# Loads of v issued from GpSimd's queue instead of SyncE's, in a fused top-k attention and Fourier-mixing kernel

## The chip, the core and the metric

The kernel runs on one core of one Trainium2 chip. A core has TensorE (PE in the profile), VectorE (DVE), ScalarE (ACT), GpSimd (POOL) and SyncE (SP). Each engine works through its own instruction queue in order and waits for the others through semaphores. PE, DVE, ACT and POOL compute; SP in this kernel only issues DMAs. The metric is the device time of one execution in microseconds (us), lower is better.

## What is computed

Inputs are q, k and v of shape (8, 8, 576, 64), that is 8 batches, 8 heads, 576 tokens and 64 channels of a head, and two weights. Cut to what matters:

```python
scores = scale * q @ k^T                        # per batch and head, 576 x 576
scores = where(scores >= 32nd largest of the row, scores, -1e9)
attn   = softmax(scores)
x      = (attn @ v), heads side by side         # (8, 576, 512)
u      = x + real(fft over channels(fft over tokens(x)))
un     = (u - mean(u)) / sqrt(var(u) + 1e-6)
out    = u + relu(un @ w_ch1) @ w_ch2           # hidden width 2048
```

All arithmetic is in float32.

## The kernel before

**Steps.** Two heads of one batch form a pair: 32 pairs, 4 of them to a batch (`NPB`). A pair has nine items (`PER_PAIR`, in the order of `IN_PAIR`), each 128 rows of scores with 576 columns; a pair's fifth item holds the leftover rows of both heads. The 288 items are run by one loop over steps `i` (line 1492). All instructions of a step are emitted in the order in which the loop meets them, and this order is the order in each engine's queue (the schedule is manual, line 1261). I call the step with `i % 9 == 7` "step 7 of a pair".

**An item's way.** VectorE finds the 32 largest values of a row in four rounds (`max`, line 425, and `match_replace`, line 427). At the end of the item's step GpSimd makes from them the two scalars `nt` (`bounds`, line 434). In the next step ScalarE forms a mask from the scores (line 448), GpSimd subtracts it from the scores (line 451), and ScalarE takes the exponential with a row sum (`expo`, line 459). From the second batch on, except in the last pair of the second batch and the last pair of all, the result goes through device memory: two ScalarE copies split its words (line 472), SP writes them out (`planes`, lines 485 and 488), and one step later SP issues a transposing DMA (`turn`, line 506) that brings them back as `PT`. TensorE multiplies `PT` with v (`attend`, line 564): a pair's first chunk four steps after its fifth item, so in step 8 of the pair; its second chunk four steps after the ninth, so in step 3 of the next pair. ScalarE then takes the product away (line 578).

**Around it.** Between these pieces the loop places the work of earlier batches: the Fourier stage (fold operations on GpSimd at lines 651 to 719; products on TensorE at lines 755, 812 and 816; ScalarE copies at lines 786 and 833; `add_mixed` on GpSimd at line 839; row statistics on VectorE at line 844; transposes on TensorE at line 881, each followed by a ScalarE copy at line 884) and the two matrix products of the channel network (TensorE lines 966, 993, 1032 and 1163; GpSimd sums at lines 1108 and 1135). A planner (`some`, `level`) spreads the TensorE part of this over the steps by estimated costs.

**The loads of v.** `v_t` holds two buffers that the pairs use in turn. `load_v(pair)` issues four DMAs, all on SP: two of 128 KB (line 288: 128 partitions, four runs of 256 bytes each) and two of 16 KB for the last 64 tokens (`load_tails`, line 255). In step 7 of a pair the loop calls `load_v` for the next pair, after the step's products and before `bounds` and the rest of GpSimd's work of the step. The first pair's v is loaded ahead of the loop. A buffer being loaded in step 7 was last read in step 3 of the same pair; what is loaded is first read in step 8 of the next pair.

**Queues around the call.** In step 7 SP's queue holds, in order: the transposing DMA of the item pair that the fifth item ends (`turn`), the write of item 5's planes, in some pairs the return of weight parts (line 909), then v's four loads, then stores if any. In step 8 follows the write of item 6's planes. GpSimd's queue holds in step 7: the subtraction of item 6, folds and sums if any, `nt` of item 7, sums, weight parts (line 923) or `add_mixed` if any. In step 8 it begins with the subtraction of item 7.

Of the kernel before, what the change touches and what calls it, by code (L numbers as in the profile page):

```python
# [73 lines left out]
def kernel(  # L74
# [9 lines left out]
    nc = tc.nc  # L84
# [11 lines left out]
    NPB = H // 2  # L96
# [129 lines left out]
    nat, qT_of, kT_of, v_of, PT, Ssb, Wk, Wp, M8, Nt = ({} for _ in range(10))  # L226
# [6 lines left out]
    def head_of(src, pair, e):  # L233
        b, hp = divmod(pair, NPB)
        return src[b, 2 * hp + e]
# [9 lines left out]
    def load_tails(dst, src, pair, queue=None, heads=(0, 1)):  # L245
        for e in heads:
            if src is q:
                for h in range(2):
                    (queue or nc.sync).dma_start(
                        out=dst[TH * h:TH * (h + 1), NF, e, :],  # L250
                        in_=head_of(src, pair, e)[HS * h + 2 * P:HS * (h + 1)],
                    )
            else:
                r0 = TAIL * e if src is v else 0
                (queue or nc.sync).dma_start(
                    out=dst[r0:r0 + TAIL, NF, e, :], in_=head_of(src, pair, e)[NF * P:S]
                )

    def load_nat(n, pair):
        if pair < NPAIR:  # L260
            nat[n, pair] = nat_t
            src = q if n == "q" else k
            b, hp = divmod(pair, NPB)
            both = src[b, 2 * hp:2 * hp + 2]
            if n == "k":
                for e in range(2):
                    nc.sync.dma_start(
                        out=nat_t[:, 0:NF, e, :],
                        in_=both[e, 0:NF * P].rearrange("(c p) d -> p c d", p=P),
                    )  # L270
                nc.sync.dma_start(
                    out=nat_t[0:TAIL, NF, :, :], in_=both[:, NF * P:S].rearrange("e r d -> r e d")
                )
                return
            for e in range(2):
                for h in range(2):
                    load_half(nat_t, src, pair, e, h)
            for h in range(2):
                nc.sync.dma_start(
                    out=nat_t[TH * h:TH * (h + 1), NF, :, :],  # L280
                    in_=both[:, HS * h + 2 * P:HS * (h + 1)].rearrange("e r d -> r e d"),
                )

    def load_v(pair):
        if pair < NPAIR:
            v_of[pair] = v_t[pair % 2]
            for e in range(2):
                nc.sync.dma_start(
                    out=v_of[pair][:, 0:NF, e, :],
                    in_=head_of(v, pair, e)[0:NF * P].rearrange("(c p) d -> p c d", p=P),  # L290
                )
            load_tails(v_of[pair], v, pair)

    def prep(n, pair, blocks=((0, NF), (NF, NC))):

# [31 lines left out]
    PER_PAIR = len(IN_PAIR)  # L327
# [4 lines left out]
    N = len(items)  # L332
# [74 lines left out]
    def top_ops(i, rounds):  # L407

        if not 0 <= i < N:
            return []  # L410
        if i not in Wk:
            e = items[i][2]
            if e != 1:

                if e is None:
                    Wp[i] = attp.tile([P, 1, S], F32, name=f"wk_{i}", tag="W1", bufs=1)
                else:
                    Wp[i] = attp.tile([P, 2, S], F32, name=f"wk_{i}", tag="W", bufs=3)
            Wk[i] = Wp[i - 1][:, 1, :] if e == 1 else Wp[i][:, 0, :]
            M8[i] = small.tile([P, TOPK], F32, name=f"m8_{i}", tag="m8", bufs=5)  # L420
        w, m, s = Wk[i], M8[i], Ssb[i]
        ops = []
        for r in rounds:
            src, m8 = s if r == 0 else w, m[:, 8 * r:8 * r + 8]
            ops.append(lambda src=src, m8=m8: nc.vector.max(out=m8, in_=src))  # L425
            if r < TOPK // 8 - 1:
                ops.append(lambda src=src, m8=m8: nc.vector.match_replace(w, m8, src, NEG))  # L427
        return ops
# [883 lines left out]
    for n in range(3):  # L1312
        load(n)
    load_v(0)
    load_nat("q", 1)
    for n in range(3, AHEAD):
# [123 lines left out]
    queue, waiting, pending, written, now, out_next = [], [], [], set(), [0], []  # L1440
    step_us = 6.0

    def chunk_at(i):

        for tile in (i - 4, i - 3, i - 2):
            r = tile % PER_PAIR
            if PER_BATCH <= tile < N and r in (4, 8):
                if i - tile == (4 if by_dma(tile) else 2 if tile == 2 * PER_BATCH - 1 else 3):
                    return tile // PER_PAIR, r // 8
        return None, None  # L1450
# [22 lines left out]
    def run(i, where):  # L1473
        for fn in plan.pop((i, where), []):
            fn()
# [15 lines left out]
    i, carry = 0, 0.0  # L1491
    while i < N + 5 or plan or queue or sums:
        now[0] = i
        run(i, "begin")
        pair_of = i // PER_PAIR
# [50 lines left out]
        if short:  # L1546
            fixed += tok
            pair, r = divmod(i - 1, PER_PAIR)
# [40 lines left out]
        pair, ch = chunk_at(i)  # L1589
# [8 lines left out]
        if i < N:  # L1598
            if q_step:
                load_nat("k", pair_of + 1)  # L1600
            if i % PER_PAIR == 5:
                load_nat("q", pair_of + 2)
            if i % PER_PAIR == 7:
                load_v(pair_of + 1)
        first, second = top_ops(i, (2, 3)), top_ops(i + 1, (0, 1))
        for n in range(max(len(first), len(second))):
            for ops in (first, second):
# [17 lines left out]
        run(i, "dve")  # L1625
        for where in ("pool", "pool2", "load", "load2"):
            run(i, where)
        late_now[:] = late_next
        late_next.clear()
        carry = max(-4.0, min(4.0, cost + got - step_us))  # L1630
# [37 lines left out]
```

## Time and profile before

| | |
|---|---|
| median of 3 runs | 1873.34 us (1872.83 to 1874.46) |
| the profiled execution's own time | 1868.68 us |
| its span, first to last instruction | 1866.9 us |
| mean granted TensorE clock | 0.955 of full speed |
| busy PE, DVE, ACT, POOL | 91%, 85%, 69%, 49% of the span |
| DMAs issued by SP for v | 64 of 128 KB and 64 of 16 KB |
| v's loads, issue to landing | 2.0 to 6.4 us |

The span has three parts. Up to about 240 us the weights arrive and the first batch's attention runs. From there to about 1690 us attention of a batch runs beside the Fourier stage and channel network of the one before; here TensorE and VectorE are both almost full (from 960 to 1200 us: 233.2 and 224.1 us busy of 240). The rest, to 1867 us, is the channel network of the last batch, almost all on TensorE. An engine's share of busy time does not tell how long others wait for it: GpSimd is busy half of the time, but a piece of each item's way lies on it.

### The profile page before, as it was taken

How to read it: one execution, taken by the hardware profiler on the slowest of the kernel's cores; microseconds unless marked ns; L12 is line 12 of the kernel's file. 1: busy time of each engine (PE TensorE's matmuls, PEld its weight loads, DVE VectorE, ACT ScalarE, POOL GpSimd, SP SyncE). 2: the span in 40 equal slices, each digit the busy share in tenths (PEclk: the TensorE clock that was granted, in tenths of full speed). 3: DMA queues.
4: the chain of work that ended last, by engine and by line, in shares of the span. 5: the costliest groups of instructions: out<-in, count | busy, mean ns of one | idle time of the engine just before them, and what ended most of it. 6: DMA issues, size and time to landing. Idle time of an engine off the chain costs nothing.

```text
span 1866.9 us, 26900 instructions
## 1 busy us (share of the span) xinstructions
PE 1704.1 (91%) x8134; PEld 1086.8 (58%) x8134; DVE 1584.9 (85%) x3301; ACT 1294.6 (69%) x3104; POOL 912.8 (49%) x1278
## 2 busy tenths in 40 slices
PE   5576699889899999899999999999999999999999
PEld 3344365365456555566556565666567555677677
DVE  7999989889899999999999899999999899762110
ACT  6878659577787778777787688767787678652100
POOL 4768644454745366354644465355545464341012
PEclk7777799899899999999999999999999999999999
DMA  5334016661567755586476755785467655530132
GB/s 168 104 92 115 20 45 162 168 176 26 129 157 202 188 128 130 147 208 160 118 169 169 188 127 139 154 230 133 128 162 189 161 121 146 133 106 6 51 112 72
DMA packets 516576, 249.16 MB, mean 133 GB/s; under 512 B 398288, under 2 KB 506448, under 8 KB 516432
## 3 DMA queue, kind: packets, MB, share of 16 engines
q1 hardware_dynamic: 515664, 247.23, 51.2%
q8 instruction: 65, 1.06, 0.2%
q14 instruction: 79, 0.65, 0.1%
q10 hardware_dynamic: 768, 0.21, 0.1%
HBM read 93.63 MB, written 84.74 MB: 96 GB/s over the span
## 4 chain that ended last, share of the span: by engine, by line
PE 61%; DVE 14%; POOL 7%; ACT 7%; DMA 4%; issue 4%; SPq 1%; POOLq 0%; DVEq 0%
PE hp L966 22%; PE cp L993 8%; PE o L564 7%; DVE m L425 6%; DVE wk L427 6%; PE sp L401 4%; PE cw L1163 4%; PE yp L755 3%; POOL wk L451 3%; PE cv L1163 3%; PE cp L1032 2%; PE sp_t L371 2%; ACT wk L448 1%; DMA PT<-planes 1%; DMA planes<-wk 1%
## 5 line engine op out<-in xcount | busy, mean ns | idle before, releaser
L451 POOL TENSOR_TENSOR wk<-S,wk 128x576 f32<-128x576 f32 x288 | 408.1, 1417 | 524.6 <-ACT wk L448 520.9
L425 DVE MAX8 m<-wk 128x8 f32<-128x576 f32 x864 | 626.8, 750 | 6.2
L966 PE MATMUL hp<-unT,w 128*128 128x256 f32 (+1 forms) x2048 | 528.3, 410 | 5.2 <-ACT unT L884 3.4
L966 PEld LDWEIGHTS hp<-unT,w 128*128 128x128 f32 x2048 | 381.3, 192 | 116.3 <-issue 10.1
L427 DVE MATCH_REPLACE8 wk<-m,wk 128x576 f32<-128x576 f32 x576 | 427.6, 742 | 0.0
L472 ACT COPY wk<-S 128x576 uint16<-128x576 uint16 x468 | 289.4, 669 | 0.0
L448 ACT ACTIVATE wk<-S,nt 128x576 f32<-128x576 f32 x288 | 223.2, 775 | 91.3 <-POOL nt L434 89.8
L564 PE MATMUL o<-PT,v 128*64 128x256 f32 (+3 forms) x1440 | 209.3, 437 | 34.7 <-DMA PT<-planes 18.6
L993 PE MATMUL cp<-w,hT 128*128 128x512 f32 x512 | 236.0, 601 | 0.0
L425 DVE MAX8 m<-S 128x8 f32<-128x576 f32 x288 | 213.8, 742 | 16.1 <-ACT S L375 16.1
L459 ACT ACTIVATE S<-wk,nt 128x576 f32<-128x576 f32 x234 | 184.5, 789 | 51.5 <-POOL wk L451 50.2
L427 DVE MATCH_REPLACE8 wk<-m,S 128x576 f32<-128x576 f32 x288 | 213.7, 742 | 0.0
L970 ACT ACTIVATE hT<-hp 128x320 f32<-128x320 f32 (+1 forms) x256 | 103.2, 411 | 146.0 <-PE hp L966 144.5
L564 PEld LDWEIGHTS o<-PT,v 128*64 128x64 f32 x1440 | 120.3, 160 | 113.4 <-issue 38.9
L401 PE MATMUL sp<-kT,qT 64*128 64x512 f32 (+1 forms) x528 | 169.0, 670 | 15.5 <-ACT S L393 7.7
L404 ACT COPY S<-sp 128x512 f32<-128x512 f32 (+1 forms) x264 | 141.8, 587 | 25.6 <-PE sp L401 24.7
L993 PEld LDWEIGHTS cp<-w,hT 128*128 128x128 f32 x512 | 93.3, 193 | 91.0 <-issue 90.5
L1108 POOL TENSOR_TENSOR hT<-hT 128x512 f32<-128x512 f32 x64 | 81.4, 1275 | 107.5 <-ACT hT L970 91.5
L434 POOL TENSOR_TENSOR nt<-m,cc 128x2 f32<-128x2 f32 x288 | 58.9, 204 | 142.0 <-DVE m L425 139.5
L371 PEld LDWEIGHTS sp_t<-kt,qT 128*128 128x128 f32 x320 | 50.6, 193 | 108.5 <-issue 69.8
L1163 PE MATMUL cw<-w,hT 128*128 128x256 f32 x448 | 104.7, 381 | 1.6 <-issue 1.6
L527 PE MATMUL tpP<-ident,wk 128*128 128x128 f32 x216 | 40.3, 318 | 58.9 <-ACT wk L459 34.1
(160 smaller groups left out, 2178.2 us busy)
## 6 DMA issues: line engine op xcount, KB each, us to landing
planes<-wk SPq DMA_DIRECT2D x208, 288.0 KB, 2.7
w<-w_parts SPq DMA_DIRECT2D x82, 512.0 KB, 4.7
space<-in_moe_w_ch_dram SPq DMA_DIRECT2D x32, 512.0 KB, 3.7
nat<-in_q_dram SPq DMA_DIRECT2D x128, 64.0 KB, 2.5
v<-in_v_dram SPq DMA_DIRECT2D x64, 128.0 KB, 3.0
out_dram<-x SPq DMA_DIRECT2D x32, 256.0 KB, 2.6
nat<-in_k_dram SPq DMA_DIRECT2D x62, 128.0 KB, 3.1
planes<-wk SPq DMA_DIRECT2D x52, 144.0 KB, 2.6
```

Of the source, the lines that this page charges most:

```text
L401: nc.tensor.matmul(sp[r], lhsT=qT[hd, q_cols], rhs=kT[hd, :], start=True, stop=True)
L404: nc.scalar.copy(out=s_t[r, keys], in_=sp[r])
L425: ops.append(lambda src=src, m8=m8: nc.vector.max(out=m8, in_=src))
L427: ops.append(lambda src=src, m8=m8: nc.vector.match_replace(w, m8, src, NEG))
L448: nc.scalar.activation(out=w, in_=Ssb[i], func=AF.Relu, scale=-FAR, bias=Nt[i][:, 1:2])
L451: nc.gpsimd.tensor_tensor(out=w, in0=Ssb[i], in1=w, op=ALU.subtract)
L459: nc.scalar.activation(out=Ssb[i] if by_dma(i) else w, in_=w, func=AF.Exp, bias=Nt.pop(i)[:, 0:1], accum_out=den_t[pair % 3][:, c:c + 1],)
L472: nc.scalar.copy(out=words[:, half, :], in_=src[:, half, :])
L564: nc.tensor.matmul(o[D * e:D * (e + 1), c0:c1], lhsT=vv[:, c, e, :], rhs=pt[:, NF if c == NF else (NF + 1) * e + c, c0:c1], start=(c == 0) ...
L966: nc.tensor.matmul(hp[:, 0:w], lhsT=w1[:, dt, P * it:P * (it + 1)], rhs=unT[:, dt, 0:w], start=(dt == 0), stop=(dt == NDT - 1),)
L993: nc.tensor.matmul(cp, lhsT=hT[:, it, P * n:P * (n + 1)], rhs=w2[:, it, :], start=(it == 0), stop=(it == NIT - 1),)
L1163: nc.tensor.matmul(dst, lhsT=h()[a][:, kc, :], rhs=rhs_of(kc), start=start and kc == 0, stop=kc == NK - 1, skip_group_check=True,)
```

## The change

From the fifth pair on `load_v` takes GpSimd's queue, and the call in the loop moves from the middle of step 7 to the end of it, behind all GpSimd work of that step. The first five pairs' v (pairs 0 to 4) still goes through SP; for pairs 1 to 4 the call is also the later one. So 27 pairs are concerned, with 4 DMAs each.

```diff
     def load_v(pair):
         if pair < NPAIR:
             v_of[pair] = v_t[pair % 2]
+            queue = nc.sync if pair <= NPB else nc.gpsimd
             for e in range(2):
-                nc.sync.dma_start(
+                queue.dma_start(
                     out=v_of[pair][:, 0:NF, e, :],
                     in_=head_of(v, pair, e)[0:NF * P].rearrange("(c p) d -> p c d", p=P),
                 )
-            load_tails(v_of[pair], v, pair)
+            load_tails(v_of[pair], v, pair, queue)
...
             if i % PER_PAIR == 5:
                 load_nat("q", pair_of + 2)
-            if i % PER_PAIR == 7:
-                load_v(pair_of + 1)
         first, second = top_ops(i, (2, 3)), top_ops(i + 1, (0, 1))
...
         for where in ("pool", "pool2", "load", "load2"):
             run(i, where)
+        if i < N and i % PER_PAIR == 7:
+            load_v(pair_of + 1)
         late_now[:] = late_next
```

The order of instructions on TensorE, VectorE and ScalarE stays the same. On SP 108 DMAs are gone. On GpSimd four DMAs stand behind the last instruction of step 7 and ahead of the subtraction of item 7, 27 times; the operations around them keep their order.

## The prediction

> **What bounds the kernel now.** I began with the stretches of the span, then took the list of waits, then the instructions in order of time around the places where v is loaded. The columns of the first view are the stretch, its length, then busy us (and instructions) of PE, PE's weight load, DVE, ACT and POOL, TensorE's granted clock, the DMA share and GB/s.
>
> ```profile
> 960.00:1200.00 240.00, 233.18 (x1122) 146.75 (x1121) 224.14 (x466) 185.60 (x441) 116.03 (x169) 0.99 0.62 158
> 1640.00:1866.00 226.00, 222.43 (x1031) 163.16 (x1027) 52.16 (x119) 46.93 (x117) 43.62 (x66) 1.00 0.20 66
> ```
>
> While attention runs, PE is 97% and DVE 93% busy, in lock step; after it PE alone. So a us by which PE or DVE is held up in the middle is a us at the end, unless PE would have waited later anyway. POOL has half its time free, but it stands in each item's way. In the waits (total us, times, longest) its idle time is time in which it waits for ACT, and ACT in turn waits for POOL:
>
> ```profile
> POOL wk L451 <- ACT wk L448: 520.9, 230, 9.3
> ACT wk L448 <- POOL nt L434: 89.8, 68, 4.0
> ACT S L459 <- POOL wk L451: 50.2, 49, 10.6
> ```
>
> The loads themselves hold up nobody. On SP no wait stands at lines 288 and 255, they land in 2.0 to 6.4 us, and they are read a whole pair (about 50 us) later. Line 1 of the next fence is from v's own view, line 2 too, line 3 from that of line 506 (min/median/max ns of one):
>
> ```profile
> L288 SPq DMA_DIRECT2D v<-in_v_dram x64: 419/562/1127, 8.0 to 1607.4; - x64
> L255 SPq DMA_DIRECT2D v<-in_v_dram x64: 513/595/773, 9.3 to 1608.6; - x64
> L506 SPq DMA_TRANSPOSE PT<-planes x130: 1294/2538/7724, 256.1 to 1629.1; - x130
> ```
>
> **What the change removes.** 27 times SP loses 2 x 0.562 + 2 x 0.595 = 2.31 us of issuing. I cost that at nothing. SP mostly waits (349.9 us for ACT's line 472, 202.6 us for planes to land). It is late behind v only in the last pair of a batch: in pair 23 v occupies SP from 1244.31 to 1246.85 and item 6's planes go out at 1246.96, although ACT had them at 1243.6. But the second chunk's last transposing DMA is issued at 1261.47, takes some 4.6 us, and the products that need it start at 1273.91: over 7 us of cover. Without that cover it would be 3.3 us a batch. One other use: in pair 5, SP sends a part of w2 (line 925) at 338.44, right after v, and POOL waits 10.8 us for it; it would come up to 2.6 us sooner.
>
> **What it adds, and where.** Four DMAs stand in POOL's queue between `nt` of item 7 and the subtraction of item 7, for which ACT's exponential waits, and behind that ACT's whole queue. Their waits (v's buffer read for the last time four steps before; the load two pairs back) are over by then. The place in pair 21, the second of its batch (start, length, engine, line, form, idle before):
>
> ```profile
> 1143.02 2.51 POOL L839 TENSOR_TENSOR x<-x,us 128x512 f32<-128x512 f32 x2
> 1145.49 1.41 POOL L451 TENSOR_TENSOR wk<-S,wk 128x576 f32<-128x576 f32 x1
> 1146.86 0.19 POOL L434 TENSOR_TENSOR nt<-m,cc 128x2 f32<-128x2 f32 x1
> 1147.78 2.52 POOL L839 TENSOR_TENSOR x<-x,us 64x512 f32<-64x512 f32 x2 [0.72 <-ACT us L833]
> ```
> ```profile
> 1148.06 0.83 ACT L459 ACTIVATE S<-wk,nt 128x576 f32<-128x576 f32 x1
> ...
> 1153.42 0.62 ACT L833 COPY us<-mp 128x512 f32<-128x512 f32 x1 [1.08 <-PE mp L816]
> ```
> ```profile
> 1153.22 0.60 PE L881 MATMUL tpu<-ident,x 128*128 128x128 f32 x4
> 1154.18 0.63 PE L881 MATMUL tpu<-ident,x 128*128 128x128 f32 x4 [0.36 <-ACT us L833]
> ```
> ```profile
> 1151.33 0.68 DVE L844 BATCH_NORM_STATS2 st<-x 64x6 f32<-64x512 f32 x1
> ```
>
> Let D be the time that the four DMAs hold POOL. In pair 21 the subtraction follows line 839 without a gap, so all of D delays it. ACT's exponential starts 1.16 us after the subtraction's end (1148.06 - 1146.90); ACT's next idle time is the 1.08 us before line 833, and PE already waits for line 833. So PE is late by D - 2.24. DVE too: the second line 839 has 0.73 us of room and line 844 follows it 1.03 us later (1150.30 to 1151.33), so DVE is late by D - 1.8. Both engines that bound are late together, and nothing later takes it up.
>
> I did the same at the other 26 places; they fall into kinds that repeat with the batch (room = POOL's gap before the subtraction + ACT's room before the exponential + ACT's idle time or the distance until PE needs a late piece):
> - Second pair of a batch (13, 17, 21, 25, 29): room 2.24.
> - First pair (12, 16, 20, 24, 28): POOL's folds follow the subtraction, and PE's line 755 needs them 3.66 us after they end; with the gap of 0.89 the room is 4.5. In pair 8 line 755 already waits for them: room 0.9.
> - Third pair (10, 14, 18, 22, 26, 30): gap 2.2, exponential 0.7, and PE's transposes of line 604 start 2.3 us after ACT's line 578: 5.2.
> - Last pair (11, 15, 19, 23, 27): 0.2 + 0.95 + ACT's idle 3.57 before line 578: 4.7. Here PE waits 2.4 to 2.8 us in step 8 for a transposing DMA, so about 2.5 us of PE's lateness is taken up once a batch.
> - Second batch and pair 9: pair 6 about 2.5 (gap 0.94, exponential 0.48, then 1.1 until PE needs a bank back); in pair 5 PE has eight products of 3.60 us in all ahead, as cover for the 2.2 us by which D exceeds the sooner w2; 4, 7 and 9 I cost at nothing, behind 2.1 to 3.7 us of gap and PE's other work. If that cover is gone, each costs what D exceeds its room by.
>
> **D.** No DMA is issued by POOL in this trace. From below: nothing, if POOL hands them off without stopping. The nearest row is the same transfers on SP, 2.31 us. From above: the longest issue among SP's kinds of DMA, the transposing one at 2.54 us, four times: 10.2. POOL is an engine that must do something else than SP's issue, and I have no row that says how much, so I take the geometric middle of the two rows: sqrt(0.578 x 2.54) = 1.21 each, D = 4.83.
>
> **The sum** at D = 4.83: second pairs 5 x 2.59 = 12.9; pair 8 3.9; first pairs 5 x 0.33 = 1.7; pair 6 2.3; last pairs 5 x 0.13, taken up. Together 20.8. Profiled execution 1868.7 + 20.8 = 1889.5; the median of the runs is 4.66 above that execution, so 1894.1.
>
> At D = 2.31: pair 8 1.4, second pairs 0.4: about 1875. At D = 0: 1873, less 2.6 if pair 5's part of w2 counts in full. At D = 10.2: second pairs 39.8, pair 8 9.3, first 28.5, third 30, last 27.5 less 2.5 a batch = 15, pair 6 7.7: 130, so 2003.
>
> **What the Trainium skill says.** Its page "DMA: Bandwidth & Descriptors", section "SWDGE vs HWDGE vs iDMA", speaks against the change: for a DMA issued from GpSimd a program on that engine writes the descriptors, and plain transfers are to go through SP or ACT. It gives a first byte after about 1 us there against 0.6. Taken as an estimate of 1 us for each issue, D would be 4.0 and the sum 8.8 + 3.1 + 1.5 = 13.4 us instead of 20.8. The trace has only SP's side, 0.56 us. The section "Issuing engines are not separate DMA queues" of the same page adds that another issuer saves only time on the sequencer, which agrees with the nothing that I gave SP's relief.
>
> **Rivals.**
> - POOL's issue is as cheap as SP's, D up to 2.9: the rooms cover it and the time stays at 1873 to 1877, say 1875. For it: POOL is 49% busy and idles 1.1 us on average right there. Against: 2.31 us is already above the room of pair 8 and at that of the second pairs.
> - The issue is dear, D of 7 and more, and POOL bounds its step in every pair: 1941 at D = 7.5 (26.3 + 6.6 + 15 + 13.8 + 1.5 + 5 = 68.2), 2003 at 10.2. For it: the larger loads are 512 runs of 256 bytes, small pieces. Against: SP's issue hardly grows from 16 KB to 128 KB (595 and 562 ns).
> - Faster: v's data competes with the transposing DMA of step 7. In the last pairs v is issued at 1244.31 and PE starts only when that DMA has landed, 1246.51, after 2.40 us of waiting; then its 20 products take 4.60 us against 2.91 elsewhere. If v's traffic makes that wait, its going gives up to 2.4 + 1.7 us in seven pairs: 29 us, 1845; it decides once D is under the 4.7 of room there. Against: the transposing DMA is issued 4.5 us ahead of v, and v would now be sent from about 1242.3, earlier, not later.
>
> **How the numbers follow.** Forecast, slower by D of 2.9 to 7: 0.45; cheap issue, no change: 0.22; dear issue: 0.23; faster: 0.10. A measurement of this kernel can tell about 0.2% (3.7 us) from no change. The time is the forecast's, 1894. The range goes down to 1870 (D = 0 with pair 5's gain), leaving out most of the faster rival, and up to 1975, at D near 9, leaving out the dear rival's last third. Faster 0.10, same 0.22, slower 0.68.
>
> **What would show it.** POOL's rows at the new lines 289 and 255, or the gap that they leave between `nt` of item 7 and the subtraction, give D. Right: POOL's line 451 in item 7 starts D less its old gap later; ACT's wait at line 459 for POOL grows from 50 us by some 27 x 3; PE waits for ACT at lines 881 and 755 in first and second pairs. Wrong: D outside 2.9 to 7; or PE's idle time growing in the last pairs; or step 8's planes going out sooner and PE's wait for `PT` shrinking, which would give SP's relief a value.

## The result, and the profile after

The changed kernel is slower by 0.42%: ratio 1.0042 to the kernel before, 95% interval 1.0030 to 1.0055. On the 1873.3 us from which the prediction started that is 7.9 us (5.6 to 10.3). Its median is 1879.87 us; its profiled execution took 1877.53 us with a span of 1875.7. Forecast were 20.8 us more, so the direction was right and the size was not.

The same views as before. First the stretches (the last one is longer because the span is):

```profile
960.00:1200.00 240.00, 233.05 (x1113) 146.46 (x1111) 222.27 (x462) 184.34 (x438) 127.98 (x188) 0.98 0.61 158
1640.00:1875.00 235.00, 231.03 (x1076) 170.39 (x1075) 60.61 (x136) 53.28 (x131) 50.67 (x74) 1.00 0.23 71
```

TensorE and VectorE are as full as before, and only POOL has gained work: over the whole span 980.9 us busy instead of 912.8, which is 68 us for 27 times four DMAs, or 2.5 a time. So the loss is not a busy engine, and the waits must show it:

```profile
POOL wk L452 <- ACT wk L449: 500.8, 213, 11.3
...
ACT wk L449 <- POOL nt L435: 83.7, 63, 4.2
...
ACT S L460 <- POOL wk L452: 65.1, 66, 10.9
...
PE o L565 <- DMA PT<-planes: 27.2, 9, 7.2
```

The last of these read before:

```profile
PE o L564 <- DMA PT<-planes: 18.6, 8, 6.6
```

Two lines grew. ACT's wait for POOL's subtraction went from 50.2 to 65.1 us. TensorE's wait for `PT` went from 18.6 us with a longest of 6.6 to 27.2 with a longest of 7.2, and part of it is put down to other engines in both lists. The first line shrank: POOL now issues DMAs where it waited.

The view of v gives D at once (min/median/max ns):

```profile
L289 POOL DMA_DIRECT2D v<-in_v_dram x54: 759/783/970, 283.7 to 1615.9; - x54
L255 POOL DMA_DIRECT2D v<-in_v_dram x54: 538/543/550, 285.4 to 1617.2; - x54
```

Two times 0.783 and two times 0.543 are 2.65 us. The place in pair 21 shows that this really holds the engine:

```profile
1142.29 2.50 POOL L840 TENSOR_TENSOR x<-x,us 128x512 f32<-128x512 f32 x2
1144.74 1.56 POOL L289 DMA_DIRECT2D v<-in_v_dram  x2
1146.29 1.07 POOL L255 DMA_DIRECT2D v<-in_v_dram  x2
1147.38 1.42 POOL L452 TENSOR_TENSOR wk<-S,wk 128x576 f32<-128x576 f32 x1
```
```profile
1148.83 0.78 ACT L460 ACTIVATE S<-wk,nt 128x576 f32<-128x576 f32 x1 [1.35 <-POOL wk L452]
```
```profile
1153.95 0.63 PE L882 MATMUL tpu<-ident,x 128*128 128x128 f32 x4 [0.36 <-ACT us L834]
```
```profile
1150.59 0.68 DVE L845 BATCH_NORM_STATS2 st<-x 64x6 f32<-64x512 f32 x1
...
1151.43 0.69 DVE L845 BATCH_NORM_STATS2 st<-x 128x6 f32<-128x512 f32 x1
```

The four DMAs stand without a gap between POOL's sums and the subtraction: from 1144.74 to 1147.36, D = 2.6 us. ACT waits 1.35 us for it, where the prediction's room gives 2.63 - 1.16 = 1.47. TensorE's transpose starts 11.95 us after item 7's `nt` (1142.00), before it was 11.45 (1142.73 to 1154.18): 0.5 us late, predicted 0.4. VectorE is not late here: the instruction that the prediction showed (64x6) starts 8.59 us after `nt`, before it was 8.60 (1142.73 to 1151.33). The prediction had it late by D - 1.8; VectorE's line comes twice and needs the two pieces of POOL's line 840 one after the other, so the room was larger.

Now the last pair of a batch, pair 27, before and after. SP's queue before, with TensorE's products that wait for `PT`:

```profile
1444.71 2.18 SPq L506 DMA_TRANSPOSE PT<-planes  x1
1446.99 0.58 SPq L485 DMA_DIRECT2D planes<-wk  x1
1447.67 0.56 SPq L909 DMA_DIRECT2D w<-w_parts  x1
1448.28 1.21 SPq L288 DMA_DIRECT2D v<-in_v_dram  x2
1449.53 1.21 SPq L255 DMA_DIRECT2D v<-in_v_dram  x2
1450.86 0.60 SPq L485 DMA_DIRECT2D planes<-wk  x1
```
```profile
1450.36 4.60 PE L564 MATMUL o<-PT,v 128*64 128x320 f32 x20 [3.11 <-DVE x L1121]
```

and after, SP, POOL and TensorE:

```profile
1449.86 1.36 SPq L507 DMA_TRANSPOSE PT<-planes  x1
1451.33 0.76 SPq L486 DMA_DIRECT2D planes<-wk  x1
1452.18 0.56 SPq L910 DMA_DIRECT2D w<-w_parts  x1
1452.86 1.25 SPq L486 DMA_DIRECT2D planes<-wk  x1
```
```profile
1450.17 1.55 POOL L289 DMA_DIRECT2D v<-in_v_dram  x2
```
```profile
1459.23 4.60 PE L565 MATMUL o<-PT,v 128*64 128x320 f32 x20 [7.21 <-DMA PT<-planes]
```

Before, the transposing DMA is issued at 1444.71 and lands 5.6 us later; TensorE waits 3.11 us (the engine named is wrong, it had long been done). After, it is issued at 1449.86 and lands 9.1 us later; TensorE waits 7.21. Between issue and landing there now lie v's loads, sent 0.3 us after it and not 3.6, and item 6's planes, sent 3.0 us after it and not 6.1, because SP no longer has v ahead of them. Summed over pairs 15, 19, 23 and 27 TensorE's wait at this place is 10.9 us before and 19.9 after: 9 us more. The two profiles differ by about as much (1875.7 - 1866.9 = 8.8), but not all of the waiting stays: followed instruction by instruction, TensorE falls 5.8 us further behind over these four places (3.1 of it in pair 27; in pair 19 it makes up 1.5). Over pairs 8 and 21 alone it falls another 3.3 and 3.6 us behind (0.5 of the latter at the place shown above). These are single profiles, which were already 2.2 us apart the other way before the first of the 27 places.

### The profile page after: what moved, and what is told of

Read it like the earlier page. It is cut to its first block, busy times and chain, and to the rows that moved or that the text cites. A ratio compares the mean times of both kernels' runs of the same rounds, so it can differ in the third digit from the quotient of the medians.

```text
span 1875.7 us, 26985 instructions
## 1 busy us (share of the span) xinstructions
PE 1705.9 (91%) x8134; PEld 1090.4 (58%) x8134; DVE 1584.3 (84%) x3301; ACT 1296.1 (69%) x3104; POOL 980.9 (52%) x1386
## 4 chain that ended last, share of the span: by engine, by line
PE 57%; POOL 12%; DVE 11%; ACT 9%; issue 5%; DMA 4%; SPq 1%; POOLq 0%; DVEq 0%
PE hp L967 23%; PE o L565 6%; DVE m L426 5%; PE cp L994 5%; DVE wk L428 5%; POOL wk L452 5%; PE sp L402 5%; PE cw L1164 4%; PE cv L1164 3%; PE cp L1033 2%; ACT wk L449 2%; PE yp L756 2%; POOL fg L652 2%; ACT wk L473 2%; PE sp_t L372 2%
## 5 line engine op out<-in xcount | busy, mean ns | idle before, releaser
L565 PE MATMUL o<-PT,v 128*64 128x256 f32 (+3 forms) x1440 | 208.1, 435 | 44.3 <-DMA PT<-planes 27.2
L460 ACT ACTIVATE S<-wk,nt 128x576 f32<-128x576 f32 x234 | 183.9, 786 | 66.5 <-POOL wk L452 65.1
```

What stands on the lines that cost most here:

```text
L460: nc.scalar.activation(out=Ssb[i] if by_dma(i) else w, in_=w, func=AF.Exp, bias=Nt.pop(i)[:, 0:1], accum_out=den_t[pair % 3][:, c:c + 1],)
L565: nc.tensor.matmul(o[D * e:D * (e + 1), c0:c1], lhsT=vv[:, c, e, :], rhs=pt[:, NF if c == NF else (NF + 1) * e + c, c0:c1], start=(c == 0) ...
```

## The experiments

There are two theories. A: POOL's hold of 2.6 us costs, through the subtraction and ACT. B: in the last pair of a batch the transposing DMA of step 7 lands later, because of what is sent beside it. The kernel before was run beside each; its medians differed from one set to the next (1868.5 to 1873.0 us), so only ratios are compared.

**POOL's hold alone.** v stays on SP; at the end of the same 27 steps POOL adds a spare tile to itself.

```diff
+    spare = const.tile([P, 192], F32, name="spare", tag="spare")
...
+        if i < N and i % PER_PAIR == 7 and NPB <= pair_of < NPAIR - 1:
+            for cols in (192, 192, 192, 192, 128):
+                nc.gpsimd.tensor_tensor(
+                    out=spare[:, 0:cols], in0=spare[:, 0:cols], in1=spare[:, 0:cols], op=ALU.add
+                )
```

> The kernel before, v still on SP, with about 2.6 us of idle additions on POOL (on a spare tile) where the changed kernel has its four DMAs, in the same 27 steps. Theory A, POOL being held is what costs: the same loss as the change, +6 to +8 us, about 1880. Theory B, v's transfers meeting the transposing DMA of step 7 in the last pair of a batch is what costs: by the rooms of the prediction only pair 8 and the second pairs lose, 1.7 + 5 x 0.4 = +3.7 at most, 1873 to 1877, and PE's wait for PT in the last pairs (2.3 to 3.1 us each) stays as it was.

```profile
1146.97 2.74 POOL L1632 TENSOR_TENSOR spare<-spare 128x192 f32<-128x192 f32 x5
1149.67 1.41 POOL L452 TENSOR_TENSOR wk<-S,wk 128x576 f32<-128x576 f32 x1
```

The hold, in POOL's order of time in pair 21 of this kernel, is 2.74 us. The ratio is 1.0024 (1.0007 to 1.0040), so +4.5 us (1.3 to 7.5). The rooms of the prediction give 2.5 + 1.85 + 0.2 = 4.6 at this D. TensorE's wait for `PT`, summed over pairs 15, 19, 23 and 27, stays at 11.3 us. A is real. By its middle value it is too small to be all of 7.9, but the intervals overlap, so this run alone does not show that there is more.

**The hold at the size that was forecast.** Eight additions of 192 columns and one of 104 in place of the five.

> As the run before, with about 4.8 us, the D that the prediction took. If the prediction's rooms are right and only D was wrong: +21 us, about 1894. If the rooms are larger than worked out (PE and DVE take more of the delay up): +5 to +12 us, 1878 to 1885. Theory B says nothing of this run.

Hold 5.03 us, ratio 1.0154 (1.0126 to 1.0182): +28.8 us (23.6 to 34.1). At D = 5.03 the prediction's rooms give 14.0 for the second pairs, 4.1 for pair 8, 2.6 for the first pairs and 2.5 for pair 6: 23. In the profile, compared with the one before from one pair's step 7 to the next (by the start of its transposing DMA), the kernel falls behind by 15.2 us after the second pairs' holds, by 4.7 after pair 8's, 1.4 after pair 6's, 1.7 after pair 16's and by 5.0 after pair 5's, which the prediction had costed at nothing. So the rooms were nearly right, a little too wide, and the loss grows steeply: by the middle values 1.8 times the hold costs 6 times as much.

**The last pairs alone.** The changed kernel, with the loads made in the last pair of a batch back on SP, and then the opposite. Both lines concern six of the 27 loads (the first text below says seven; the seventh, of pair 4, is on SP in the changed kernel too).

```diff
-            queue = nc.sync if pair <= NPB else nc.gpsimd
+            queue = nc.sync if pair <= NPB or pair % NPB == 0 else nc.gpsimd
```
```diff
-            queue = nc.sync if pair <= NPB else nc.gpsimd
+            queue = nc.gpsimd if pair > NPB and pair % NPB == 0 else nc.sync
```

> The changed kernel, but v that is loaded in the last pair of a batch goes through SP again (7 of the 27 loads), at the end of the step. Theory A: the loss lies in pair 8 and the second pairs, so nothing changes, 1879 to 1881. Theory B: nearly all of the loss is gone, 1873 to 1876, and PE waits 2.3 to 3.1 us for PT in the last pairs, not 3.4 to 7.2.

> The opposite: only the loads made in the last pair of a batch go through POOL (6 loads), the others through SP at the end of the step. Theory A: the rooms of the last pairs (4.7 us) cover 2.63 us, so 1872 to 1875. Theory B: the loss is here, 1877 to 1881.

Without the last pairs' loads POOL's queue costs 1.0023 (1.0006 to 1.0039), with them alone 1.0036 (1.0018 to 1.0054). The first is neither theory's number: it is A's part, as in the hold alone, and B's is gone. The second is B's: six loads, a fifth of all, cost 6.7 us (3.4 to 10.1), in a place whose room on POOL is 4.7 us against a hold of 2.6. The landing of `PT` around pair 27 tells the two apart. Each line has three transposing DMAs, of which step 7's is one: first with these loads on SP, where step 7's is the middle value, 5.0 us; then with these alone on POOL, where it is the largest, 8.8:

```profile
DMA to landing us min/median/max: 4.6/5.0/5.2
```
```profile
DMA to landing us min/median/max: 4.5/4.7/8.8
```

The same for all kernels (landing of step 7's transposing DMA in us, and TensorE's wait for it):

| v of the last pairs on | kernel | pair 15 | 19 | 23 | 27 | PE's waits, sum |
|---|---|---|---|---|---|---|
| SP | before | 3.3 | 5.5 | 6.6 | 5.6 | 10.9 |
| SP | hold of 2.74 us | 3.4 | 4.9 | 6.8 | 5.2 | 11.3 |
| SP | hold of 5.03 us | 3.5 | 5.4 | 6.7 | 5.1 | 10.8 |
| SP | other pairs on POOL | 3.4 | 5.0 | 6.8 | 5.0 | 10.9 |
| POOL | changed | 6.6 | 5.9 | 8.0 | 9.1 | 19.9 |
| POOL | last pairs alone | 4.7 | 6.0 | 8.6 | 8.8 | 19.3 |

The two kernels also issue their loads on SP at the end of step 7 and not in the middle. With transposing DMAs no run has that difference alone, but in the traces it hardly moves them: where the last pairs alone are on POOL, the others' v leaves SP within 0.4 us of where it did before, counted from the transposing DMA, in all but three of the 21 pairs.

In the other pairs of the changed kernel v on POOL does not make the DMA late: with v sent 0.9 to 2.7 us after it, it lands after 3.6, 3.4 and 3.4 us in pairs 29, 21 and 25, as before. What the four last pairs have besides is the return of weight parts: one to three loads of 512 KB that SP issues 2 to 3 us ahead of the transposing DMA, and one or two more behind it. Pair 11, a last pair without these loads, has the DMA landing after 3.5 us with v on POOL and 3.4 with v on SP. Pair 10, a third pair, has one such load ahead: 4.3 us with v on POOL, but also 4.2 with v on SP and the hold of 2.74 us. No run takes the weight loads away to try this.

**Without a transposing DMA.** All pairs take the way of the first batch, where TensorE turns the exponentials and ScalarE copies them; the rest stays, and the same values are computed.

```diff
     def pair_by_dma(pair):
-        return NPB <= pair < NPAIR - 1 and pair != 2 * NPB - 1
+        return False
```

> The kernel before with every pair's exponentials turned by TensorE and ScalarE (the way that the first batch, pair 7 and pair 31 take in the kernel before) in place of planes and transposing DMA; v on SP in step 7. A base for the three runs beside it. Some 232 items more with 4 or 5 transposes on PE at about 0.6 us: 1980 to 2050 us, PE bounding more than before.

> The same without transposing DMA, v as in the changed kernel (POOL, end of step 7, 27 loads). Theory A (POOL's hold of 2.63 us): slower than the run with v on SP by 2 to 8 us. Theory B (the transposing DMA is late): its part is gone, so whatever is left of the loss is A's; none, within 3 us, if PE bounds so much that the rooms on POOL and ACT have grown.

> Without transposing DMA, only the loads made in the last pair of a batch on POOL. Theory B: no loss against the run with all of v on SP at the end of the step, within 3 us, where the same edit with transposing DMAs cost 0.36%. If it costs 5 to 9 us here too, the loss of the last pairs doesn't come through the transposing DMA.

> Without transposing DMA, all of v on SP at the end of step 7: the move without the queue. Within 3 us of the run with the call in the middle of the step, if the place on SP is free.

All against the kernel before: v on SP in the middle of step 7 1.0288 (1.0267 to 1.0308), all on SP at the end of it 1.0293 (1.0272 to 1.0313), the last pairs' on POOL 1.0283 (1.0263 to 1.0304), all 27 on POOL 1.0304 (1.0282 to 1.0327). The base, 1923.6 us, is well under the 1980 expected: the transposes cost less than was taken. The last pairs' loads on POOL now cost nothing against the run with all on SP (-0.1%), where they cost 0.36% with the transposing DMAs. So their loss comes by way of those DMAs or of the writes of the planes that belong to them, which these kernels don't have either; the table's waits are for the DMAs. The move to the end of the step costs nothing that these runs can tell. All 27 loads on POOL cost 0.16%, with intervals that overlap: A's part, not sure by itself.

**What POOL's time for a DMA is made of.** The kernel without transposing DMA and with all 27 loads on POOL, each large load cut into four of 32 KB, so ten DMAs a pair.

```diff
             for e in range(2):
-                queue.dma_start(
-                    out=v_of[pair][:, 0:NF, e, :],
-                    in_=head_of(v, pair, e)[0:NF * P].rearrange("(c p) d -> p c d", p=P),
-                )
+                for c in range(NF):
+                    queue.dma_start(
+                        out=v_of[pair][:, c, e, :],
+                        in_=head_of(v, pair, e)[c * P:(c + 1) * P],
+                    )
```

> Without transposing DMA, v on POOL as in the changed kernel, but each large load cut into four of 32 KB (128 runs of 256 bytes each), so ten DMAs a pair in place of four. If POOL's time for a DMA is a fixed part and a part for each run, by the line through 543 ns for 64 runs and 783 ns for 512: 577 ns each, 5.7 us of hold a pair, and 1.5 to 3 times the loss of the run with four DMAs against the one with v on SP. If the time goes by bytes or runs alone: 196 ns each, 2.6 us of hold, the same time as with four.

```profile
L290 POOL DMA_DIRECT2D v<-in_v_dram x216: 534/537/758, 285.0 to 1682.8; - x108
L255 POOL DMA_DIRECT2D v<-in_v_dram x54: 520/530/537, 289.5 to 1683.9; - x54
```

A DMA of 128 runs holds POOL for 537 ns, one of 64 for 530, one of 512 for 783: about 0.53 us however small, and 0.25 more for the largest. Ten DMAs are 5.4 us of hold. The ratio is 1.0398 (1.0368 to 1.0428), 1.1% above the run with v on SP, by the middle values seven times what four DMAs cost and not 1.5 to 3 times. What four cost is itself not clear of noise, but a loss that grows faster than the hold agrees with the second experiment.

## Why the prediction was right or wrong

- **What bounds the kernel**: right. TensorE and VectorE stay full, POOL's extra work is not what is paid for, and what is paid for are waits behind it.
- **D = 4.83, the geometric middle of SP's issue and the transposing DMA's**: this is the term that failed. It measured 2.63. The value lay beside the nearest row, the same transfers on SP (2.31 us), and the transposing DMA, another kind of work, said nothing about it. By its own table the prediction gives 2.0 + 1.7 + 0.1 = 3.8 us at the true D, that is the rival that it called cheap issue (D up to 2.9, 1875 us). (The middle of its two rows is 4.85, not 4.83; nothing hangs on it.) A D outside 2.9 to 7 and more waiting of TensorE in the last pairs were the signs that it had named for being wrong, and both came.
- **The rooms**: right in the main. A hold of 2.74 us cost 4.5 (4.6 by the table), one of 5.03 us 28.8 (23 by it). In detail VectorE's lateness in the second pairs did not come, and pair 5's cover did not hold: alone the hold cost 5.0 us there. In the changed kernel pair 5 lost nothing; there SP sends its part of w2 without v ahead of it, the 2.6 us that the prediction named, but that this is the reason was not tried by itself.
- **SP's relief costed at nothing, and the faster rival**: wrong in sign. The prediction saw that v's data and the transposing DMA of the last pairs meet, gave the meeting to a gain, and wrote as the argument against it that v "would now be sent from about 1242.3, earlier, not later". It did not price that sentence. It is the other part of the loss: the DMA lands 0.4 to 3.5 us later in those pairs, TensorE waits 9 us more in all, and 4.7 us of room on POOL's side did not matter, since the wait does not pass through POOL. The gain was also over-counted: the wait of 2.4 us and more stands in four last pairs before the change (2.4 to 3.1 us), not in seven.
- **The last pairs' 2.5 us that are taken up**: not used in the end, as D stayed under the room there and the wait grew instead.
- **The rule of the Trainium skill** ("DMA: Bandwidth & Descriptors", section "SWDGE vs HWDGE vs iDMA") that plain loads belong on SP or ACT pointed the right way. The estimate of 1 us an issue, from the page's figure for the first byte, was above what the trace shows (0.54 and 0.78).

Two small losses, POOL's hold with 0.24% and the last pairs with 0.36% when each is alone, make the 0.42% of the change within their intervals. That both are there is shown; how the 0.42% divides between them is not.

**What stays open.** In the last pairs two things came at once: v's data are sent by POOL while the transposing DMA is under way, and item 6's planes are written 2 to 3 us sooner, since SP is free. No run separates them. Two places of the traces point at v's data. In pair 15 the planes leave 4.1 us after the DMA (3.9 with the last pairs alone), and with v on SP the DMA had landed after 3.3 to 3.5, so a write sent that late cannot be what first held it up. And in pair 29, which has no weight loads, v was once sent 0.2 us after the DMA (the kernel with the other pairs on POOL) in place of 0.9 (the changed kernel), with the planes 2.1 us after it both times: it landed after 4.5 us in place of 3.6. In pairs 23 and 27, where most of the delay is, either could be the cause. A kernel that keeps v on SP and issues it one step later would tell, and might beat both; no run here has it.

## What to carry to other kernels

Price an instruction that no row shows by the nearest row, and keep the far one for the range only: the loss here sets in at a threshold, and less than twice the hold was some six times the price. An engine with half its time free can still be the wrong issuer if something waits for its next instruction within a few us. And if a change frees a queue, list what moves up in it, and which transfer in flight that meets.

## What was not expected of the hardware

The transposing DMA of step 7, which lands in 3.3 to 3.6 us in most pairs, took 4.9 to 6.8 behind two or three loads of 512 KB and up to 9.1 with v's 288 KB on another queue beside it and a planes write sooner behind it. After such a wait TensorE can pay a second time. In pair 23 of the kernel before, after 2.40 us, the 20 products take 4.60 us at a granted clock of 0.63; in the kernel with the hold of 5.03 us, after 2.58 us at the same place, they take 2.91 at 1.00. So a wait of this length does not by itself bring the lower clock; what decides it these runs do not show.
